# A third buffer for raw weight chunks and a shifted pace of decoding

## The chip, the core and the metric

The kernel runs on one core of a Trainium2 chip. The metric is the device time of one execution in microseconds; a kernel's time is the median over several executions. The engines are named as in the profile: PE is the matrix engine (PEld its weight loads), DVE the vector engine, ACT the scalar engine, POOL the GpSimd engine, SP the engine whose queue issues nearly all of this kernel's DMAs.

## The reference

Two blocks follow one another. Four batches of eight heads, 768 positions, 64 dimensions; a query sees the keys of its own cluster only; then a feed-forward layer with a hard-swish gate over 3072 tokens.

```python
def _attn_ref(q, k, v, centroids):
    q_n, k_n, c_n = ...                     # rows divided by their norms
    q_assign = np.argmax(np.einsum('bhsd,hcd->bhsc', q_n, c_n), axis=-1)
    k_assign = np.argmax(np.einsum('bhsd,hcd->bhsc', k_n, c_n), axis=-1)
    mask = q_assign[:, :, :, None] == k_assign[:, :, None, :]
    scores = scale * np.matmul(q, k.transpose(0, 1, 3, 2))
    scores = np.where(mask, scores, -1000000000.0)
    attn = np.exp(scores - np.max(scores, axis=-1, keepdims=True))
    attn = attn / (np.sum(attn, axis=-1, keepdims=True) + 1e-09)
    return np.matmul(attn, v)

def _moe_ref(x, w_in, w_out):               # (3072,512) (512,2048) (2048,512)
    h = x @ w_in
    g = h * np.clip(h + 3.0, 0.0, 6.0) / 6.0
    return g @ w_out
```

The weights `w_in` and `w_out` arrive as 64-bit floating-point numbers. The kernel reads them as pairs of 32-bit words and makes 32-bit floats of them: this is the decoding of which the change speaks.

## The kernel before

The heads are worked on in 16 pairs. A pair has 12 steps `n` (two halves of the queries, six chunks of keys in each), and the program's loop takes two steps at a time, so that `r = n % 12` is 0, 2, 4, 6, 8 or 10. The order of the instructions on each engine is the order in which this loop writes them out (`tc.manual_schedule`); semaphores between the engines are added to it. A batch is four pairs, 48 steps.

In each step PE forms the scores of 128 keys and 384 queries for two heads (`ps`, L418), ACT takes the exponentials (`ex`, L441), POOL sums them over the keys (`acc`, L461 and L464), and two steps later PE multiplies them with v (`pv`, L474). Once in six steps `divide` has PE add up the sums into one PSUM bank (`pd`, L495), DVE take the reciprocal (`rcp`, L499) and the product (`num`, L500). Then `keep` stores the result to DRAM (`xd`, L503) and lets ACT run the two activations of `in_range` over `rcp` (L512, L513); they come out one loop turn later. The preparation of the next pair lies between: transposes of q and k (`pqk`, copied to `xf`), scores against the centroids (`pcs`, copied to `cs`), their maximum and the one-hot rows on DVE (`mx` L337, `one_hot` L343), and the transposed one-hots (`po`, copied to `xm`). One PSUM pool, `psum_t`, has a single bank; from step 96 on `pd`, `pcs` and the other scratch tiles of the preparation share it.

The weights are 32 chunks of 128 x 512 numbers. `load_weights(i)` requests one chunk on SP's queue into a tile `raw` of pool `rawp` (L208). Five operations decode it: `split` (which also requests a further chunk, starts an activation on ACT that reads `raw`, L221, and a shift on DVE, L225), `join` (L231), `power` (a second activation, L237, and L241), `rest` (the last reader of `raw` on DVE, L247) and `total` (L252). After 160 of these come eight `weight_sums` (L547), which form sums of blocks of `w_out` for a fast matrix product after Strassen and Winograd. At the end of every turn of the loop, `share(n, r)` says how many of these 168 operations are written out:

```python
for step in decode[: share(n, r)]:
    step()
del decode[: share(n, r)]
```

`READY` is 56 and `DECODED` is 96. From step 60 to step 94 eight `up` items of the feed-forward layer are put in (`ph`, L613 on PE; ACT's `lift`, L523; DVE's `clip`, L526; four POOL sums of the results, L648). They read `xb`, a block that SP loads back from `xd` (L561). From step 96 on the decoding is over, four steps are written out together, and the first `down` items form the products `X` and `Y` (L693), along with which `make_first_sums` writes sums of `w_in` (`tx`, L580) on DVE.

All of this is the program's fast path. A general path for inputs outside its assumptions follows behind a branch; with these inputs it isn't run.

Of the kernel before, what the change touches and what calls it, by code (L numbers as in the profile page):

```python
# [116 lines left out]
def fast_path(ctx, tc, ok, q, k, v, centroids, moe_w_in, moe_w_out, out):  # L117
# [23 lines left out]
    dram = pool("dram", 1, space=bass.MemoryType.DRAM)  # L141
    yp = pool("yp", 1)
    decoding = ctx.enter_context(ExitStack())
    rawp = decoding.enter_context(tc.tile_pool(name="rawp", bufs=2))
    decp = decoding.enter_context(tc.tile_pool(name="decp", bufs=2))
    startp = decoding.enter_context(tc.tile_pool(name="startp", bufs=1))
    psum_s = pool("psum_s", 2, space=PSUM)
# [26 lines left out]
    def scratch(shape, name, dtype=F32):  # L174

        if st["early"]:
            return psum_m.tile(shape, dtype, name=name, tag="m")
        return psum_t.tile(shape, dtype, name=name, tag="t")
# [3 lines left out]
    def load(g, *names):  # L182
        if g >= NPAIR:
            return
        b, h = divmod(2 * g, H)
        for name in names:
            if name == "v":
                dst = st["v", g] = vp.tile([P, 2, NCH, D], F32, name="vt")
            elif name == "q":
                st["qk", g] = qkp.tile([P, 2, NCH, 2, D], F32, name="qk")  # L190
            if name != "v":
                dst = st["qk", g][:, "qk".index(name)]
            src = {"q": q, "k": k, "v": v}[name]
            for t in range(2):
                nc.sync.dma_start((dst[:, t] if name == "v" else dst[:, :, t]), src[b, h + t].rearrange("(p j) d -> p j d", p=P))
# [9 lines left out]
    def load_weights(i):  # L205
        if i < len(chunks):
            st["raw", i] = rawp.tile([P, WC, 2], U32, name="raw")
            nc.sync.dma_start(st["raw", i], chunks[i][1])  # L208

    def decoding_steps(i):  # L210

        got = {}

        def split():
            load_weights(i + 1)
            raw = st.pop(("raw", i))
            got.update(lo=raw[:, :, 0], hi=raw[:, :, 1])
            got["size"] = decp.tile([P, WC], BF16, name="wsize")
            got["top"] = psum_t.tile([P, WC], U32, name="wtop", tag="t")
            got["unit"] = decp.tile([P, WC], U32, name="wunit")  # L220
            nc.scalar.activation(  # L221
                out=got["size"], in_=got["hi"].bitcast(F32), func=ACT.Abs,
                accum_out=w_totals[:, 0, i : i + 1],
            )
            nc.vector.tensor_scalar(  # L225
                out=got["top"], in0=got["hi"], scalar1=3, scalar2=0x3FFFFFFF,
                op0=ALU.logical_shift_left, op1=ALU.bitwise_and,
            )

        def join():  # L230
            nc.vector.scalar_tensor_tensor(  # L231
                out=got["top"], in0=got["hi"], scalar=0xC0000000, in1=got["top"],
                op0=ALU.bitwise_and, op1=ALU.bitwise_or,
            )

        def power():
            nc.scalar.activation(  # L237
                out=got["size"], in_=got["size"], func=ACT.Relu, bias=w_low, scale=-1.0,
                accum_out=w_totals[:, 1, i : i + 1],
            )  # L240
            nc.vector.tensor_scalar(  # L241
                out=got["unit"], in0=got["top"], scalar1=0xFF800000, scalar2=None, op0=ALU.bitwise_and
            )

        def rest():
            unit = got["unit"].bitcast(F32)
            nc.vector.scalar_tensor_tensor(  # L247
                out=unit, in0=got["lo"], scalar=2.0**-52, in1=unit, op0=ALU.mult, op1=ALU.mult
            )

        def total():
            nc.vector.tensor_tensor(  # L252
                out=chunks[i][0], in0=got["top"].bitcast(F32), in1=got["unit"].bitcast(F32), op=ALU.add
            )

        return [split, join, power, rest, total]
# [8 lines left out]
    def constants():  # L265
        make_identity(nc, ident)
        for t in range(2):
            nc.vector.tensor_reduce(
                out=parity[:, t : t + 1],
                in_=ident.rearrange("p (h t c) -> p t h c", t=2, c=C)[:, t], axis=AX.XY, op=ALU.max,  # L270
            )
        nc.gpsimd.memset(half_c, 0.5)
        nc.gpsimd.memset(low_c, 1.0 / BOUND)
        nc.gpsimd.memset(ones, 1.0)
        nc.gpsimd.memset(w_low, W_LOW)
        nc.gpsimd.memset(one_hot, 0.0)
        for c in range(C):
            nc.gpsimd.memset(number[:, c : c + 1], float(c))

        warm = psum_t.tile([P, 4, P], F32, name="warm", tag="t")  # L280
        for i in range(14):
            nc.tensor.transpose(out=warm[:, i % 4], in_=ident, identity=ident)
# [36 lines left out]
    def cluster_scores(g):  # L319
        c0, xf = (2 * g) % H * C, st["xf", g]  # L320
        ps = scratch([P, 512], "pcs")[:, 0 : NC2 // 4 * P]
        for a in range(4):
            nc.tensor.matmul(  # L323
                ps[a * 2 * C : (a + 1) * 2 * C], lhsT=cnT[:, c0 : c0 + 2 * C], rhs=xf[:, a::4],
                start=True, stop=True,
            )
        cs = st["cs", g] = rtp.tile([P, NC2 // 4, P], F32, name="cs")
        nc.scalar.copy(out=cs, in_=ps)
# [81 lines left out]
    def scores_qk(n):  # L410
        st["ps", n] = psum_s.tile([P, 2, 512], F32, name="ps")
        scores_part(n, st["xf", where(n)[0]], True, by_vector(n))
# [402 lines left out]
    def share(n, r):  # L815

        if n < READY:
            return {0: 4, 2: 2, 4: 3, 6: 1, 8: 2, 10: 4}[r]
        return {0: 6, 2: 5, 4: 5, 6: 3, 8: 5, 10: 5}[r]

    def items_by(n):

# [56 lines left out]
    with tc.manual_schedule():  # L879
        nc.scalar.dma_start(cen, centroids.rearrange("h c d -> (h c) d"))  # L880
        load(0, "q", "k")
        constants()
        load(0, "v")
        load_weights(0)
        centroid_norm()
        for part in range(3):
            turn(0, part)
        centroid_turn()
        nc.vector.tensor_copy(out=ident_q, in_=ident)
        load(1, "q", "k")  # L890
        cluster_scores(0)
        scores_qk(0)
        route(0)
        scores_qk(1)
        for part in range(2):
            route_turn(0, part)

        for n in range(0, total + lag_d + 2, 2):
            g, r = divmod(n, per_pair)
            fours = n >= DECODED  # L900
            steps = [i for i in (n, n + 1) if i < total]
            prep = prep_items(g + 1, r, fours)
            if fours:
                four_by_four(n, r, steps)
            else:
                for i in steps:
                    scores(i)
                    exponentials(i)
                    key_sums(i)
                for i in (n - lag_v, n - lag_v + 1):  # L910
                    if i >= 0:
                        attn_v(i)
                m = n - lag_d + 1
                if m >= 0 and m % NCH == NCH - 1:
                    later.append(divide(m))
                    ready(m)
            if prep and r == (6 if fours else 4):
                prep.pop(0)()
            if n == DECODED:
                st["early"] = False  # L920
            if r == 6 and not fours:
                load(g + 2, "q", "k")
                load(g + 1, "v")
            if not fours or r % 4 == 2 or n >= total:
                want = min(items_by(n + 2) - st["done"], len(fill))
                st["done"] += want
                for i in range(max(len(prep), want)):
                    if i < want:
                        fill.pop(0)()
                    if i < len(prep):  # L930
                        prep[i]()
            if r == 6 and fours:
                load(g + 2, "q", "k")
                load(g + 1, "v")
# [3 lines that stand above are left out]
            if not fours:  # L938
                for op in numbers:
                    op()  # L940
                numbers.clear()
                check_all()
            checks.extend(later)
            later.clear()

        while checks:
            check_all()
            checks.extend(later)
            later.clear()
        st["last"] = True  # L950
        flag = whether_good()
        while fill:
            fill.pop(0)()
            if len(fill) == HOLD // 2:
                flag()
# [363 lines left out]
```

## Time and profile before

| | us |
|---|---|
| median of 8 runs | 1013.88 |
| lowest and highest | 1012.55, 1015.71 |
| the profiled execution | 1013.33 |
| its span, first to last instruction | 1011.5 |
| PE busy in the span | 987.9 |
| DVE, POOL, ACT busy | 564.3, 430.9, 390.2 |

Start and idle times in the text are microseconds from the start of the span. The profile comes from one execution. A wait is named after the instruction that waited and the one whose end released it. Busy times of PE include pipelining, so a PE that is busy throughout is not necessarily at its peak.

### The profile page before, as it was taken

How to read it: one execution, taken by the hardware profiler on the slowest of the kernel's cores; microseconds unless marked ns; L12 is line 12 of the kernel's file. 1: busy time of each engine (PE TensorE's matmuls, PEld its weight loads, DVE VectorE, ACT ScalarE, POOL GpSimd, SP SyncE). 2: the span in 40 equal slices, each digit the busy share in tenths (PEclk: the TensorE clock that was granted, in tenths of full speed). 3: DMA queues.
4: the chain of work that ended last, by engine and by line, in shares of the span. 5: the costliest groups of instructions: out<-in, count | busy, mean ns of one | idle time of the engine just before them, and what ended most of it. 6: DMA issues, size and time to landing. Idle time of an engine off the chain costs nothing.

```text
span 1011.5 us, 16735 instructions
## 1 busy us (share of the span) xinstructions
PE 987.9 (98%) x6560; PEld 734.6 (73%) x6560; DVE 564.3 (56%) x1085; ACT 390.2 (39%) x764; POOL 430.9 (43%) x363
## 2 busy tenths in 40 slices
PE   7999999999999999999999999999999999999997
PEld 4444445555688777788787777778777899999996
DVE  4888888988954255236236247147156372727270
ACT  6788877665233243233323333333223020201010
POOL 4877766665426326426415426515426130303030
PEclk9999999999999999999999999999999999999999
DMA  7334455432252052123223125023033041414120
GB/s 184 99 117 134 124 166 148 137 116 59 102 169 84 9 154 76 47 89 86 64 86 103 42 69 138 26 76 103 21 91 92 31 145 38 130 50 118 52 63 25
DMA packets 87560, 92.70 MB, mean 92 GB/s; under 512 B 53936, under 2 KB 68272, under 8 KB 87472
## 3 DMA queue, kind: packets, MB, share of 16 engines
q1 hardware_dynamic: 87328, 91.51, 31.4%
q8 instruction: 54, 0.88, 0.4%
q14 instruction: 34, 0.28, 0.1%
q10 hardware_dynamic: 144, 0.03, 0.0%
HBM read 75.79 MB, written 15.73 MB: 90 GB/s over the span
## 4 chain that ended last, share of the span: by engine, by line
PE 88%; DVE 6%; ACT 4%; issue 1%; DMA 1%; SPq 0%; ACTq 0%; DVEq 0%
PE Y L693 16%; PE uY L658 15%; PE ps L418 13%; PE X L693 12%; PE uX L658 12%; PE pv L474 11%; PE ph L613 2%; PE pd L495 2%; PE pqk L310 2%; DVE tx L580 1%; PE pcs L323 1%; ACT ex L441 1%; PE po L367 1%; DVE rcp L499 1%; ACT xm L369 1%
## 5 line engine op out<-in xcount | busy, mean ns | idle before, releaser
L464 POOL TENSOR_TENSOR acc<-acc,ex 128x768 f32<-128x768 f32 x128 | 241.6, 1887 | 130.9 <-ACT ex L441 124.2
L648 POOL TENSOR_TENSOR g_sb<-g_sb 128x256 f32<-128x256 f32 x176 | 127.9, 748 | 319.5 <-DVE g_sb L526 298.3
L441 ACT ACTIVATE ex<-ps 128x768 f32<-128x768 f32 x192 | 148.3, 804 | 85.1 <-PE ps L418 84.5
L523 ACT ACTIVATE sx<-g_sb,half_c 128x512 f32<-128x512 f32 x88 | 63.5, 722 | 268.3 <-DVE g_sb L669 268.3
L418 PE MATMUL ps<-xf 64*128 64x384 f32 x768 | 157.0, 487 | 0.8 <-ACT ex L441 0.8
L474 PE MATMUL pv<-ex,vt 128*64 128x384 f32 x768 | 141.1, 496 | 0.0
L700 DVE TENSOR_TENSOR y<-y,Y 128x256 f32<-128x256 f32 x48 | 20.2, 420 | 169.9 <-PE Y L693 169.1
L474 PEld LDWEIGHTS pv<-ex,vt 128*64 128x64 f32 x768 | 48.7, 136 | 82.4 <-issue 72.7
L499 DVE RECIPROCAL rcp<-pd 128x384 f32<-128x384 f32 x32 | 81.8, 2557 | 47.7 <-PE pd L495 46.8
L461 POOL TENSOR_TENSOR acc<-ex 128x768 f32<-128x768 f32 x32 | 59.6, 1861 | 99.6 <-ACT ex L441 99.6
L658 PE MATMUL uX<-xb,w_in_sb 128*128 128x128 f32 x704 | 93.0, 275 | 0.0
L693 PE MATMUL X<-w_out_sb,g_sb 128*128 128x256 f32 x384 | 89.7, 381 | 0.0
L693 PE MATMUL Y<-T,g_sb 128*128 128x256 f32 x384 | 87.3, 380 | 0.0
L693 PE MATMUL Y<-w_out_sb,g_sb 128*128 128x256 f32 x384 | 87.2, 380 | 0.0
L658 PEld LDWEIGHTS uX<-xb,w_in_sb 128*128 128x128 f32 x704 | 85.7, 192 | 0.0
L418 PEld LDWEIGHTS ps<-xf 64*128 64x128 f32 x768 | 67.7, 188 | 21.7 <-issue 18.0
L693 PEld LDWEIGHTS X<-w_out_sb,g_sb 128*128 128x128 f32 x384 | 71.2, 190 | 12.9 <-issue 3.5
L693 PEld LDWEIGHTS Y<-T,g_sb 128*128 128x128 f32 x384 | 72.3, 190 | 11.2 <-issue 1.7
L693 PEld LDWEIGHTS Y<-w_out_sb,g_sb 128*128 128x128 f32 x384 | 72.2, 190 | 11.1 <-issue 1.1
L526 DVE SCALAR_TENSOR_TENSOR g_sb<-sx,g_sb 128x512 f32<-128x512 f32 x88 | 67.3, 770 | 0.9 <-ACT sx L523 0.9
L418 PE MATMUL ps<-xm 64*128 64x384 bf16 x384 | 60.9, 327 | 6.5 <-ACT ex L441 3.4
L669 DVE TENSOR_TENSOR g_sb<-uY,sx 128x128 f32<-128x128 f32 (+1 forms) x176 | 65.6, 415 | 0.1
(110 smaller groups left out, 1379.5 us busy)
## 6 DMA issues: line engine op xcount, KB each, us to landing
tx<-td SPq DMA_DIRECT2D x86, 384.0 KB, 3.2
raw<-in_moe_w_in_dram SPq DMA_DIRECT2D x16, 512.0 KB, 4.0
raw<-in_moe_w_out_dram SPq DMA_DIRECT2D x16, 512.0 KB, 3.6
qk<-in_q_dram SPq DMA_DIRECT2D x32, 192.0 KB, 4.4
qk<-in_k_dram SPq DMA_DIRECT2D x32, 192.0 KB, 4.7
vt<-in_v_dram SPq DMA_DIRECT2D x32, 192.0 KB, 3.8
xd<-num SPq DMA_DIRECT2D x32, 192.0 KB, 2.9
xb<-xd SPq DMA_DIRECT2D x12, 512.0 KB, 4.2
```

The costliest lines, as they stand in the source:

```text
L418: nc.tensor.matmul(st["ps", n][:, t, 0:HALF], lhsT=x[r, NCH + j], rhs=x[r, hf * NHC : (hf + 1) * NHC], start=first, stop=last,)
L441: nc.scalar.activation(out=ex, in_=sc, func=ACT.Exp, scale=SM_SCALE)
L461: nc.gpsimd.tensor_tensor(out=acc, in0=st["ex", n - 1], in1=ex, op=ALU.add)
L464: nc.gpsimd.tensor_tensor(out=acc, in0=acc, in1=ex, op=ALU.add)
L474: nc.tensor.matmul(pv[t * D : (t + 1) * D], lhsT=vt[:, t, j], rhs=ex[:, t], start=(j == 0), stop=(j == NCH - 1),)
L499: nc.vector.reciprocal(out=rcp, in_=pd)
L523: nc.scalar.activation(out=r, in_=h, func=ACT.Relu, bias=half_c, scale=1.0 / 6.0)
L526: nc.vector.scalar_tensor_tensor(out=g, in0=r, scalar=1.0, in1=h, op0=ALU.min, op1=ALU.mult)
L648: eng.tensor_tensor(out=out_, in0=in0, in1=in1, op=op)
L658: nc.tensor.matmul(dst, lhsT=w[:, kt], rhs=x(kt), start=(kt == 0), stop=(kt == HK - 1))
L669: nc.vector.tensor_tensor(out=out_, in0=in0, in1=in1, op=ALU.add)
L693: nc.tensor.matmul(bank[:, half * HC : (half + 1) * HC], lhsT=g_sb[:, kind, i], rhs=w[:, i], start=(first and i == 0), stop=(last and i == ...
```

## The change

`rawp` gets a third buffer. `split` of chunk i requests chunk i + 2 instead of i + 1, and chunk 1 is requested before the loop, behind the q and k of pair 1. A request still waits until the chunk that last held its buffer has been read: that was chunk i - 1 before and it is chunk i - 1 now, but the chunk requested is needed five operations later than before. In the table of `share`, a pair has 17 operations instead of 16 before `READY` (one more at r = 2) and 28 instead of 29 from there on (one fewer at r = 4).

```diff
-    rawp = decoding.enter_context(tc.tile_pool(name="rawp", bufs=2))
+    rawp = decoding.enter_context(tc.tile_pool(name="rawp", bufs=3))
...
         def split():
-            load_weights(i + 1)
+            load_weights(i + 2)
             raw = st.pop(("raw", i))
...
         if n < READY:
-            return {0: 4, 2: 2, 4: 3, 6: 1, 8: 2, 10: 4}[r]
-        return {0: 6, 2: 5, 4: 5, 6: 3, 8: 5, 10: 5}[r]
+            return {0: 4, 2: 3, 4: 3, 6: 1, 8: 2, 10: 4}[r]
+        return {0: 6, 2: 5, 4: 4, 6: 3, 8: 5, 10: 5}[r]
...
         load(1, "q", "k")
+        load_weights(1)
         cluster_scores(0)
```

## The prediction

> **What bounds the kernel now.** I read the busy times first, then TensorE's own waits, then the chain of waits backwards from the two longest of them.
>
> ```profile
> PE 987.9 (98%) x6560; PEld 734.6 (73%) x6560; DVE 564.3 (56%) x1085; ACT 390.2 (39%) x764; POOL 430.9 (43%) x363
> ```
>
> PE is the bound, so a change outside PE pays only where PE stands idle. These are PE's waits between 10 and 290 us (total, times, longest):
>
> ```profile
> PE ps L418 <- ACT ex L441: 4.2, 6, 2.0
> PE ps L418 <- ACT xm L369: 2.8, 5, 1.3
> PE pcs L323 <- DVE rcp L499: 2.5, 1, 2.5
> PE pqk L310 <- ACT xf L312: 1.6, 2, 0.8
> ```
>
> The page's list for the whole span has the same totals, so after 290 us there is nothing of this kind. The decoding ends near 250 us. The timeline of PE places the waits (start, duration, and in brackets the idle time before):
>
> ```profile
> 191.03 0.34 PE L418 MATMUL ps<-xm 64*128 64x384 bf16 x2 [0.42 <-ACT ex L441]
> 229.96 0.34 PE L418 MATMUL ps<-xm 64*128 64x384 bf16 x2 [2.01 <-ACT ex L441]
> 271.54 0.85 PE L323 MATMUL pcs<-xf,cnT 128*32 128x384 f32 x8 [2.52 <-DVE rcp L499]
> ```
>
> The one at 229.96 is followed back in the chain of waits:
>
> ```profile
> 220.21 2.23 DVE wunit L247
> 222.50 3.83 DMA raw<-in_moe_w_out_dram
> 226.35 0.78 ACT wsize L221 x2
> ```
>
> The last raw chunk (31) could be requested only when `rest` of chunk 29 had freed its buffer at 222.45. It landed at 226.33, and ACT, which had reached this chunk's `split` at 221.35, stood still for 5.00 us, with the exponentials of step 90 queued behind it. From there DVE sets the pace:
>
> ```profile
> 231.60 0.69 DVE L526 SCALAR_TENSOR_TENSOR g_sb<-g_sb,ph 128x512 f32<-128x512 f32 x1 [2.61 <-ACT g_sb L523]
> 233.33 1.61 DVE L247 SCALAR_TENSOR_TENSOR wunit<-raw,wunit 128x512 f32<-128x512 uint32 x1
> 235.70 2.00 DVE L547 TENSOR_TENSOR T<-w_out_sb 128x1024 f32<-128x1024 f32 x1
> 242.72 4.62 DVE L547 TENSOR_TENSOR T<-w_out_sb,T 128x1024 f32<-128x1024 f32 x4
> 247.86 2.35 DVE L547 TENSOR_TENSOR w_out_sb<-w_out_sb 128x1024 f32<-128x1024 f32 x2
> 268.94 2.55 DVE L499 RECIPROCAL rcp<-pd 128x384 f32<-128x384 f32 x1
> ```
>
> Between 231.6 and 271.5 DVE has no idle time worth naming; PE was through with its work at 269.02 and waits for that reciprocal to give back its PSUM bank. So the reciprocal's end at 271.49 decides: time won upstream only lengthens this wait unless the DVE chain ends earlier too.
>
> **The change part by part.** The pace. Counting the tables, 145 decoding operations are out by step 82 (before: 142), 160 by step 88 (158), 163 by step 90 (161), and the last of the 168 at step 92 instead of 94. Nothing is added or removed; PE's order is the same.
>
> First five pairs (to 130 us): one operation more per pair, 0.73 us of DVE (starts of L225 to L231) and a fifth of ACT's 1.5 us per chunk. DVE idles about 2 us before the reciprocal of step 8 in each pair (waiting for `pd`), which covers it; uncovered it would cost 0.73 us a pair. I take 0.
>
> ACT, places where it holds PE. PE waits 0.42, 0.57 and 0.42 us (124.91, 158.91, 191.03) where step 4 of a pair issues both activations of a chunk, with the two of `in_range` behind them and then the exponentials. After the change step 52 and step 64 still have two; step 76 has one. One activation with its read is 0.7 to 0.8 us, more than 0.42: gain 0.42. Steps 22 (two for one, at r=10) and 72 (three for two, at r=0) get heavier, but before had two at steps 34 and 46 and three at step 84 without a PE wait of this kind: 0, at worst 0.57 each.
>
> The third buffer. Chunk 31 is now requested at step 84's `split` of chunk 29 and waits for `rest` of chunk 28, which in the new order stands before the clip at 211.3; it lands by about 215. ACT wants it near 219. The 5.00 us of ACT vanish; PE had been idle 2.01 of them: gain 2.01. The other DMA wait of ACT (1.07 us at 135.58) had no PE wait behind it: 0. On SP, each load still waits for the same kind of release as before, and behind it queue q, k, v loads, `xd` stores and the load of `xb` (issued 129.2). The release that counts there, at step 50, has one decoding operation more ahead of it: 0.7 us. `xb` takes 3.9 to 5.1 us and is wanted at 137.15, so some 3 us of slack cover it; beyond them every us is a us of PE. At the start, chunk 2 is requested at about 11 us instead of 17.7, just behind the k of pair 1. At the 289 GB/s seen there its 0.52 MB take 1.8 us; if all of it fell upon k, PE would lose up to 1.8 us near 15 us. As the k requests are in front, I take 0.
>
> The DVE chain, which decides. After the clip at 211.3 (now 210.9, PE being 0.42 ahead) come 6 decoding operations (4.4), reciprocal and product (2.57 + 1.30), 5 operations with one slow `rest` (5.1) and the last 4 (2.9 to 4.5): chunk 31 is finished at 227.8 to 229.4. `ph` is there at 227.15 and ACT, no longer held, lifts it by 227.8. Clip, maximum and one-hots take 1.7: the first weight sum starts at 229.6 to 231.2, against 235.70, 4.5 to 6.1 us earlier. Then three sums stand ahead of the reciprocal of step 92 instead of one: 2.00 + 2 x 1.155 (4.62/4) = 4.3; reciprocal and product 4.0; five sums 5.8; clip 0.6. That gives 244.3 to 245.9 for the first `tx` instruction, against 250.13.
>
> What may spoil it is POOL, with its sums of exponentials in the same stretch:
>
> ```profile
> 232.58 4.03 POOL L464 TENSOR_TENSOR acc<-acc,ex 128x768 f32<-128x768 f32 x2
> 236.79 4.46 POOL L464 TENSOR_TENSOR acc<-acc,ex 128x768 f32<-128x768 f32 x2 [0.18 <-ACT ex L441]
> 254.05 3.87 DVE L580 TENSOR_TENSOR tx<-w_in_sb,tx 128x256 f32<-128x256 f32 x2
> ```
>
> The first sum took 2.00 in there and 1.21 alone; the `tx` pair at 254.05 took 1.93 each where 0.43 is usual, one POOL sum apiece. But the two sums at 247.86 ran at full speed (2.35) while POOL's four L648 additions, started at 248.02, took 5.71 instead of 3.25: there POOL waited. Low end: only the first sum pays, as above. High end: all three pay a whole POOL sum, 3 x (1.89 + 1.21) = 9.3 instead of 4.3, and the 5.0 us eat the lead. I take the low end, because the neighbouring sums don't need each other's result, as those at 247.86, while each `tx` needs the one before.
>
> [...]
>
> From 244.3–245.9 the `tx` work runs on as before; POOL's pair that slowed it at 264 follows PE's exponentials and comes 2.4 earlier, when DVE is nearly through. So the reciprocal ends at 265.7 to 267.3 or sooner (its `pd` is ready at 262.3). PE arrives at 269.02 - 2.43 = 266.6. Of the 2.52 us, 0 to 0.7 remain; I take 0.2: gain 2.3. What is late next: in the new order the last clip stands behind all eight sums; PE wants its POOL products near 251.0 and they come by 247 to 249. After that PE is the bound as before.
>
> Sum: 0.42 + 2.01 + 2.3 = 4.7 us. The profiled execution took 1013.33 us (span 1011.5), so 1008.6; it lies 0.55 below the median of 1013.88, from which I forecast 1009.2.
>
> **The rivals.**
>
> A. Part is given back: the three sums delay reciprocal and product of step 92, whose `in_range` on ACT (242.40, with PE's lead 240.0) then waits, exponentials behind it; or pieces of the bounds above (k at the start, steps 22 and 72) come true. For it: the product ends at 237.9 to 239.5 in my sum, at up to 241.4 if one sum more pays. Cost 1.5 to 2.5, gain 2.2 to 3.2: about 1011.1.
>
> B. The DVE chain doesn't shift (high end of the POOL price): PE's 2.43 is lost at the reciprocal, whose wait grows from 2.52 to about 4.9. 1013.9. For it: the `tx` row at 254.05. Against: the row at 247.86, and 2.3 us of decoding that leave the chain.
>
> C. Slower. The mechanism: three sums ahead of step 92's reciprocal, each behind a POOL sum, without a lead of the decoding (if DVE's earlier waits, 3.76 us before 211.3 and 2.61 before 231.6, are not filled). The first sum then starts at 233.4, three take 9.3, the reciprocal ends at 245.3, product, five sums and clip at 253.1, 3.0 later than 250.13, and so is the reciprocal at 268.94. It decides once the first `tx` starts after 250.2. 1016.9. Against: DVE has operations ready for those waits.
>
> That the buffer does nothing is no rival of weight: the load of chunk 31 hangs on a release 11 us earlier.
>
> **How the numbers follow.** Forecast 0.65, A 0.16, B 0.11, C 0.08. Two microseconds are 0.2%, about what a measurement of this kernel can tell from no change. Faster: 0.65 and most of A, 0.78; same: B and a little of A, 0.14; slower: C, 0.08. The forecast's own range goes from 1007.8 (4.95 us gained, 0.4 for one of PE's waits for `xm` or `xf` closing too, 0.7 for the spread of a median) to 1010.2. A reaches to 1011.7; with half a microsecond of spread the whole range is 1007.8 to 1012.2, and B and C, 0.19, are left out.
>
> **What would show it.** Right: no wait of ACT for raw near 226; PE waits at 191 and 230 gone; first sum near 230; pcs L323 waiting under 0.7 us near 267. Wrong: the pcs wait at 2.5 us or more (B); sums at 2 to 3 us each with POOL between (A, B); a PE wait behind L512 near 240 (A); waits for q, k or `xb` near 15 or 137 us.

## The result, and the profile after

The changed kernel takes 1011.93 us (median of 12 runs, 1011.14 to 1013.14) beside 1014.62 us for the kernel before (32 runs, 1011.78 to 1016.72): ratio 0.9978, 95% interval 0.9968 to 0.9987. It is faster, by 2.2 to 2.7 us where 4.7 were forecast. The profiled execution took 1011.50 us, its span 1009.6 (before: 1013.33 and 1011.5). Executions of one kernel differ by some us, for two reasons given at the end, so traces are compared over one stretch: from the first `ps` of step 54, where PE waits 0.4 us in every kernel (124.91 before, 124.89 after), to the first `uX` (283.12 and 281.08). That stretch takes 158.21 us before and 156.19 after, 2.02 less; behind it PE's waits are the same in both.

The busy times after (engine, us, share of the span):

```profile
PE 988.4 (98%) x6560; PEld 734.1 (73%) x6560; DVE 568.9 (56%) x1085; ACT 390.1 (39%) x764; POOL 431.1 (43%) x363
```

PE is still the bound. DVE is 4.6 us busier with the same 1085 instructions: some of them ran slower. PE's waits between 10 and 290 us (total, times, longest):

```profile
PE ps L418 <- ACT xm L369: 2.5, 4, 1.3
PE po L367 <- DVE rcp L499: 2.2, 2, 1.8
PE ps L418 <- ACT ex L441: 1.7, 4, 0.6
PE pqk L310 <- ACT xf L312: 1.6, 2, 0.8
PE pqk L310 <- DVE rcp L499: 0.7, 1, 0.7
```

The wait for `ex` fell from 4.2 to 1.7 and the 2.5 of `pcs` are gone. New are three waits for a reciprocal, under `po` and `pqk`. PE's timeline places them:

```profile
183.30 0.66 PE L310 MATMUL pqk<-ident,qk 128*128 128x128 f32 x4 [0.73 <-DVE rcp L499]
...
199.39 0.49 PE L367 MATMUL po<-ident_q,one_hot 128*128 128x128 bf16 x6 [0.40 <-DVE rcp L499]
...
241.73 0.49 PE L367 MATMUL po<-ident_q,one_hot 128*128 128x128 bf16 x6 [1.83 <-DVE rcp L499]
```

Neither `po` nor `pqk` reads `rcp`. They want a PSUM bank: up to step 96 `scratch` takes its tiles from `psum_m`, which has two banks, and `pd` keeps one of them until the reciprocal has read it (e9 below puts this to the test for step 92). Compared point by point along PE, the trace gives this ledger (change of PE's lead in us, idle time and the restart behind it):

| place before / after | what happens | us |
|---|---|---|
| 191 / - | wait for `ex` behind step 76 gone | -0.49 |
| 230 / - | wait for `ex` behind ACT's wait for chunk 31 gone | -2.07 |
| 271 / - | wait of `pcs` for `rcp` of step 98 gone | -2.58 |
| 203 and 243 | two waits for `ex` and `xm` shorter or gone | -0.36 |
| - / 183 | `pqk` waits for `rcp` of step 74 | +0.93 |
| - / 199 | `po` waits for `rcp` of step 80 | +0.56 |
| - / 242 | `po` waits for `rcp` of step 92 | +1.99 |
| sum | | -2.02 |

So 5.5 us were gained and 3.5 given back. ACT's timeline shows the 5.00 us of waiting for chunk 31 gone (nothing in brackets):

```profile
218.99 0.66 ACT L221 ACTIVATE wsize<-raw 128x512 bf16<-128x512 f32 x1
```

DVE's timeline in the stretch that decided before:

```profile
229.26 0.69 DVE L526 SCALAR_TENSOR_TENSOR g_sb<-g_sb,ph 128x512 f32<-128x512 f32 x1 [0.51 <-ACT g_sb L523]
...
230.99 5.46 DVE L547 TENSOR_TENSOR T<-w_out_sb 128x1024 f32<-128x1024 f32 x2
236.38 2.83 DVE L547 TENSOR_TENSOR T<-w_out_sb,T 128x1024 f32<-128x1024 f32 x1
239.13 2.54 DVE L499 RECIPROCAL rcp<-pd 128x384 f32<-128x384 f32 x1
...
248.46 0.42 DVE L580 TENSOR_TENSOR tx<-w_in_sb 128x256 f32<-128x256 f32 x1
...
265.32 2.56 DVE L499 RECIPROCAL rcp<-pd 128x384 f32<-128x384 f32 x1 [1.24 <-PE pd L495]
```

The first weight sum starts at 230.99 instead of 235.70. But the three sums ahead of the reciprocal run to 239.13, 8.1 us, with POOL's sums of exponentials beside them all the time:

```profile
230.81 4.57 POOL L464 TENSOR_TENSOR acc<-acc,ex 128x768 f32<-128x768 f32 x2 [3.33 <-ACT ex L441]
235.59 5.28 POOL L464 TENSOR_TENSOR acc<-acc,ex 128x768 f32<-128x768 f32 x2 [0.22 <-ACT ex L441]
```

`pd` was ready at 232.6 and PE wanted its bank back at 239.9; the reciprocal began at 239.13 and gave it at 241.67. The last reciprocal, of step 98, is through at 267.9 and PE comes to `pcs` only at 269.51.

### The profile page after: what moved, and what is told of

Same layout as the page of the kernel before. It is cut to its first block, busy times and chain, and to the rows that moved or that the text cites. A ratio compares the mean times of both kernels' runs of the same rounds, so it can differ in the third digit from the quotient of the medians.

```text
span 1009.6 us, 16725 instructions
## 1 busy us (share of the span) xinstructions
PE 988.4 (98%) x6560; PEld 734.1 (73%) x6560; DVE 568.9 (56%) x1085; ACT 390.1 (39%) x764; POOL 431.1 (43%) x363
## 4 chain that ended last, share of the span: by engine, by line
PE 76%; DVE 2%; ACT 1%; issue 0%; ACTq 0%
PE Y L693 17%; PE uY L658 15%; PE X L693 12%; PE uX L658 12%; PE ps L418 9%; PE pv L474 7%; PE pd L495 1%; PE pqk L310 1%; PE ph L613 1%; PE pcs L323 1%; PE po L367 1%; DVE T L547 1%; DVE g_sb L526 0%; DVE sx L669 0%; DVE one_hot L343 0%
## 5 line engine op out<-in xcount | busy, mean ns | idle before, releaser
L648 POOL TENSOR_TENSOR g_sb<-g_sb 128x256 f32<-128x256 f32 x176 | 126.2, 738 | 320.3 <-DVE g_sb L526 299.0
```

What stands on the lines that cost most here:

```text
L648: eng.tensor_tensor(out=out_, in0=in0, in1=in1, op=op)
```

## The experiments

Theory: the forecast's gains are real, and the new tables give part back, as `rest` and weight sums that run beside POOL come ahead of three reciprocals, each of which holds one of two PSUM banks. Rivals: the late reciprocals hold PE up another way (`in_range` on ACT, rival A of the prediction); the sums are slow for another reason than POOL; one part of the change makes the other superfluous. Ratios below are to the kernel before in the same series, with 95% intervals; "stretch" is the time defined above.

| kernel | median us | ratio | stretch us |
|---|---|---|---|
| the change | 1011.93 | 0.9978 (0.9968 to 0.9987) | 156.19 |
| the change again (e8) | 1013.64 | 0.9987 (0.9975 to 1.0000) | 157.85, 1.65 of it slow clock |
| buffer alone (e1) | 1009.12 | 0.9943 (0.9927 to 0.9959) | 153.54 |
| buffer alone again (e11) | 1009.26 | 0.9943 (0.9928 to 0.9959) | 153.53 |
| tables alone (e2) | 1013.71 | 0.9993 (0.9983 to 1.0002) | 157.91, 1.41 of it slow clock |
| one sum ahead of step 92 (e3) | 1011.51 | 0.9961 (0.9946 to 0.9976) | 154.48 |
| steps 74 and 80 relieved (e4) | 1010.51 | 0.9960 (0.9945 to 0.9976) | 156.57, 1.61 of it slow clock |
| both (e5) | 1010.51 | 0.9949 (0.9933 to 0.9965) | 153.21 |
| without POOL's sums (e6) | 1011.99 | 0.9970 (0.9959 to 0.9981) | 154.49 |
| another bank for `pd` (e9) | 1012.32 | 0.9975 (0.9965 to 0.9986) | 155.00 |
| buffer, step 76, first try (e7) | 1009.21 | 0.9949 (0.9936 to 0.9962) | 153.56 |
| buffer, step 76 (e10) | 1008.71 | 0.9935 (0.9919 to 0.9951) | 153.10 |

"Slow clock" is what the way from PE's wait near 242 to `uX` takes over the 39.35 us of the first profile of the change. The intervals of the buffer alone, e5, e7 and e10 lie clear of that of the change; for the other kernels the times don't decide, and the readings below rest on one trace each.

**The buffer alone (e1, and again e11).** Against the changed kernel:

```diff
-            return {0: 4, 2: 3, 4: 3, 6: 1, 8: 2, 10: 4}[r]
-        return {0: 6, 2: 5, 4: 4, 6: 3, 8: 5, 10: 5}[r]
+            return {0: 4, 2: 2, 4: 3, 6: 1, 8: 2, 10: 4}[r]
+        return {0: 6, 2: 5, 4: 5, 6: 3, 8: 5, 10: 5}[r]
```

> The changed kernel with the old table of decoding operations (16 and 29 to a pair): the third buffer alone. My theory: the changed kernel wins 4.9 us at three waits of PE (191, 230, 271 us) and gives 3.0 back at three new waits for a late reciprocal, whose PSUM bank in psum_m PE wants (0.73 at 183, 0.40 at 199, 1.83 at 242 us). The first two come from where the new pace lays the slow rest operations, the third from three weight sums ahead of the reciprocal of step 92. With the old pace only one sum stands there, so none of the three new waits appears; the wait for raw (2.01 at 230) is gone, the 0.42 at 191 stays, and at 271 between 0.5 and 2.5 us are left, as two decoding operations stay in the DVE chain. Total 2 to 4 us faster than before, as fast as the changed kernel or up to 1.5 us faster. Rival (the pace does the work, the buffer is of no account): the wait at 230 stays near 2 us and the total is that of before. Rival (the buffer itself costs, by its early loads): a new wait of PE before 130 us.

> The third buffer with the old tables once more, on the same chip as the changed kernel. Theory 1 (the shifted pace gives back some 3 us): ratio 0.9935 to 0.9955, lower than that of the changed kernel by 0.002 to 0.003; 153.4 to 153.7 us from the first ps of step 54 to the first uX. Theory 2 (the first series differed by chip or by the pace of TensorE's start): a ratio within 0.001 of that of the changed kernel.

Measured: the old pace with the third buffer is the faster kernel, on two chips at the same ratio, with an interval that doesn't meet that of the change. Its stretch is 4.67 and 4.68 us shorter than before: 2.07 and 2.58 from the places at 230 and 271. PE's waits in the second of these profiles:

```profile
PE ps L418 <- ACT xm L369: 2.8, 5, 1.3
PE ps L418 <- ACT ex L441: 2.2, 5, 0.6
PE pqk L310 <- ACT xf L312: 1.6, 2, 0.8
PE po L367 <- DVE one_hot L343: 0.3, 1, 0.3
```

No reciprocal is among them. The gain is larger than expected for e1 (5.2 us against 2 to 4), as nothing of the wait at 271 is left, and the ratio lies 0.0044 below that of the changed kernel, more than the 0.002 to 0.003 expected for e11. What follows: nearly the whole gain is the buffer's, and the tables take some 2.6 us of it away.

**The tables alone (e2).** Against the changed kernel, two buffers and a request one chunk ahead:

```diff
-    rawp = decoding.enter_context(tc.tile_pool(name="rawp", bufs=3))
+    rawp = decoding.enter_context(tc.tile_pool(name="rawp", bufs=2))
...
-            load_weights(i + 2)
+            load_weights(i + 1)
...
-        load_weights(1)
```

> Two buffers and a request one chunk ahead as before, with the changed tables alone. Theory 1 (the tables alone already do away with ACT's wait for chunk 31, so that in the changed kernel the buffer no longer matters): chunk 31 is requested when `rest` of chunk 29 has ended, near 215.8 us instead of 222.45, lands by 219.6, ACT wants it at 219.0 and waits 0.6 us at most; the three PE waits for a late reciprocal (near 183, 199 and 242 us; 0.7, 0.4 and 1.8 us) stand as in the changed kernel; from the first ps of step 54 to the first uX 156.0 to 156.6 us (before 158.21, changed 156.19); ratio to the kernel before 0.997 to 0.999. Theory 2 (the buffer is what takes the wait away): ACT waits for raw by 3 us or more and PE by 1.5 us or more behind it, and with the three reciprocal waits the kernel is at 1.000 to 1.003.

Measured: ACT's activation of chunk 31 has no wait at all (its timeline), and PE's three waits for a reciprocal stand, the last of them as long as in the change:

```profile
222.18 0.68 ACT L221 ACTIVATE wsize<-raw 128x512 bf16<-128x512 f32 x1
```

```profile
244.73 0.49 PE L367 MATMUL po<-ident_q,one_hot 128*128 128x128 bf16 x6 [1.83 <-DVE rcp L499]
```

Theory 1 holds. Decoding two operations earlier brings the request of chunk 31 forward by itself, so each part of the change removes the same 5.00 us of ACT. Together they gain it once, and pay for the tables. Without the 1.41 us of slow clock the stretch would be 156.5 us, in theory 1's range; the ratio of the medians is just above it.

**Which operations hold the reciprocals (e3, e4, e5).** The changed kernel with single steps of the table set by hand: e3 has one operation instead of three at step 90, so one weight sum ahead of the reciprocal of step 92; e4 moves `join` and `power` of chunk 24 from step 72 to 74 and `rest` and `total` of chunk 26 from 78 to 80, behind the reciprocals there; e5 does both.

```diff
+        moved = {90: 1}                               # e3
+        moved = {72: 4, 74: 7, 78: 1, 80: 7}          # e4
+        moved = {72: 4, 74: 7, 78: 1, 80: 7, 90: 1}   # e5
+        if n in moved:
+            return moved[n]
```

> The changed kernel with one decoding operation instead of three at step 90, so that one weight sum stands ahead of the reciprocal of step 92 instead of three, and the two others behind it (two come out at step 94, behind the last clip, as before). My theory (bank held by a late reciprocal): the reciprocal starts near 233 instead of 239.1, PE's wait at 242 (1.83) is gone, those at 183 and 199 stay; the pcs wait near 270 stays under 0.6. 1.3 to 2.0 us faster than the changed kernel. Rival (the DVE chain decides as a whole): DVE has the same work up to 265, so the 1.8 us come back as the pcs wait near 268, and the total is that of the changed kernel within 0.5. Rival (ACT's in_range behind the product): same time gain, but then PE's wait would have been put down to ACT, and ACT shows no wait at L512 in the changed kernel.

> The changed kernel with two decoding operations moved from step 72 to step 74 and two from step 78 to step 80, that is from ahead of a reciprocal to behind it; the lead at all other steps is the same. My theory: the reciprocals of steps 74 and 80 start 1.4 to 3 us earlier (180.7 to about 179, 196.8 to about 195), PE's waits at 183 (0.73) and 199 (0.40) are gone, that at 242 stays. 0.9 to 1.2 us faster than the changed kernel, if no wait of ACT comes up by three activations at step 74. [...] Rival (the DVE chain decides as a whole): the lateness comes back at the clip of step 84 or at 242, no gain.

> Both edits in one: operations moved behind the reciprocals of steps 74, 80 and 92. My theory: the three new waits of PE are gone, the three gains stay; 2.4 to 3.2 us faster than the changed kernel, 4.5 to 5.5 faster than before. This is the 4.7 us of the prediction, got by another way. Rival (DVE chain as a whole): no more than e3 or e4 alone, the rest coming back as the pcs wait near 267.

Measured: in e3 the wait near 242 is gone and those of 0.76 and 0.39 us for steps 74 and 80 stay; in e4 these two are gone and 1.84 stays; in e5 all three are gone. The stretch is 154.48, 156.57 less 1.61, and 153.21 us. What follows: each wait hangs on the work that DVE has ahead of that reciprocal, and they add up. By the rows the reciprocals of steps 74 and 80 came late by `rest`: of the five between 170 and 197 us three take 2.13, 2.17 and 1.97 us in the change (175.74, 188.08, 194.18), each begun 0.2 to 0.4 us behind one of POOL's sums (175.51, 187.87, 193.78); before, none of the five takes over 1.17. That POOL made these slow is read from the rows and not shown by a run: e4 takes other work out of the way at step 74 and leaves the slow `rest` in its place (2.15 us in e5, which has the same operations there). The medians of e4 and e5 are equal, 1010.51; there the traces decide, not the times.

**POOL left out (e6).** Against the changed kernel:

```diff
-        elif j > 1:
+        elif j > 1 and not 92 <= n < 96:
```

> The changed kernel with POOL's four additions of exponentials (L464) of steps 92 to 95 left out; the sums of those keys are so left out of the result. Theory 1 (POOL's additions make the three weight sums slow, and these the reciprocal late): the three L547 sums ahead of the reciprocal of step 92 take 3.5 to 4.4 us together instead of 8.29, the reciprocal ends near 237.5 instead of 241.67, PE's wait of 1.83 us for it at 241.73 is gone, from the first ps of step 54 to the first uX 154.2 to 154.7 us instead of 156.19; ratio 0.995 to 0.9965. Theory 2 (the sums are slow for another reason, or the wait isn't theirs): sums at 7 us or more, the wait at 1.5 us or more, 156 us, ratio 0.997 to 0.9985.

Measured, on DVE's timeline:

```profile
233.54 2.35 DVE L547 TENSOR_TENSOR T<-w_out_sb 128x1024 f32<-128x1024 f32 x2
235.81 1.22 DVE L547 TENSOR_TENSOR T<-w_out_sb,T 128x1024 f32<-128x1024 f32 x1
236.95 2.55 DVE L499 RECIPROCAL rcp<-pd 128x384 f32<-128x384 f32 x1
```

The same three sums take 3.4 us instead of 8.1, PE's 1.83 us are gone and the stretch is 154.49 us, in theory 1's range. The ratio, 0.9970, is 0.0005 above its range, at the lower end of theory 2's, and doesn't decide. The 4.7 us are POOL's.

**Another bank (e9).** Against the changed kernel; no instruction moves:

```diff
-        pd = scratch([P, 512], "pd")
+        pd = psum_t.tile([P, 512], F32, name="pd", tag="t") if n == 89 else scratch([P, 512], "pd")
```

(`divide` counts by its last key step, 89, which is the call in step 92.)

> The changed kernel with `pd` of step 92 alone in the bank of psum_t, which is free by then, instead of one of the two banks of psum_m. No instruction is added, removed or moved. Theory 1 (PE waits at 241.73 only because `pd` holds one of the two banks that `po` needs): the three sums take 8 us and more as before, the reciprocal still ends at 241.5 to 241.8, but PE's 1.83 us are gone or under 0.2; PE then reaches pcs of step 98 near 267.7, as that reciprocal ends at 267.9, and waits 0.1 to 0.5 there; from the first ps of step 54 to the first uX 154.4 to 154.9 us instead of 156.19; ratio 0.995 to 0.997. Theory 2 (the late reciprocal holds something else up too, such as the activations of `in_range` and the exponentials behind them): a PE wait of 1 us or more stays near 242, named after another releaser; 155.7 us or more, ratio 0.997 to 0.9985.

Measured, on DVE's, ACT's and PE's timelines (all of this execution is 1.14 us later than in the change):

```profile
240.31 2.54 DVE L499 RECIPROCAL rcp<-pd 128x384 f32<-128x384 f32 x1
```

```profile
243.48 0.52 ACT L512 ACTIVATE rcp<-rcp 128x384 f32<-128x384 f32 x1 [0.98 <-DVE num L500]
```

```profile
240.91 0.50 PE L367 MATMUL po<-ident_q,one_hot 128*128 128x128 bf16 x6
...
245.58 0.34 PE L418 MATMUL ps<-xm 64*128 64x384 bf16 x2 [0.45 <-ACT ex L441]
```

The reciprocal is as late as ever (240.31 less 1.14 is 239.17), and `po` no longer waits: the bank was what held PE. Behind it a second, shorter way shows: `in_range` waits 0.98 us for the product, the exponentials stand behind it, and PE loses 0.45; a wait of 0.30 for `xm`, which the kernel before has there too, is back as well. So the stretch is 155.00, 0.1 above theory 1's range, and both theories have a part: the bank first, ACT's way of rival A next in line. The ratio, 0.9975, lies in theory 2's range and doesn't separate this kernel from the change.

**The wait behind step 76 (e7, e10).** With the buffer alone one wait of the forecast's sum remains, 0.42 us at 191. Against the buffer alone:

```diff
+        moved = {76: 4, 78: 4}   # e7
+        moved = {76: 3, 78: 5}   # e10
+        if n in moved:
+            return moved[n]
```

> The third buffer with the old tables, and one decoding operation moved from step 76 to step 78, so that step 76 issues one activation less. Theory 1 (the old tables with the buffer leave only PE's wait of 0.42 us behind step 76, and nothing takes its place): that wait under 0.1, no PE wait for a reciprocal, from the first ps of step 54 to the first uX 153.0 to 153.3 us (the buffer alone 153.54); ratio 0.9935 to 0.9950. Theory 2 (the operation moved delays the reciprocal behind it): a PE wait of 0.3 to 0.7 us for rcp near 185, 153.5 to 154.0 us, ratio 0.9945 to 0.9960.

> The third buffer with the old tables, and two decoding operations moved from step 76 to step 78, so that step 76 issues one activation instead of two (the single operation moved in the run before was `rest`, which has no activation). Theory 1 (the second activation is what PE waits for behind step 76): the wait of 0.41 us is gone, no PE wait for a reciprocal comes up, from the first ps of step 54 to the first uX 153.0 to 153.3 us (the buffer alone 153.54); ratio to the kernel before 0.993 to 0.995. Theory 2 (the wait there hangs on `in_range` and the exponentials alone, or the two operations come back as a wait behind step 78): a PE wait of 0.3 us or more between 189 and 201 us, 153.4 to 154.0 us, ratio 0.9940 to 0.9955.

Measured: e7 kept the wait (0.43 us), since the operation moved was `rest`, and the step still issued two activations: a miss of the experiment's edit. In e10, with one activation in step 76, the wait is gone, nothing takes its place, and the stretch is 153.10 us, 0.43 less than with the buffer alone. This is the fastest kernel of all, 0.9935; its time alone doesn't separate it from the buffer alone.

**The two kernels once more (e8, e12).**

> The changed kernel once more, on the same chip as the buffer alone. Theory 1: ratio 0.9965 to 0.9985, and 156.1 to 156.3 us from the first ps of step 54 to the first uX, or up to 1.6 us more where the granted clock falls behind PE's wait near 242. Theory 2: a ratio within 0.001 of the buffer alone.

> The kernel before once more, for a second profile. Three of the four profiles in which PE waits 1.83 us near 242 us show a granted clock of 0.58 to 0.66 over the four microseconds behind it, and some 1.5 us lost; none of the eight without that wait does. Theory 1 (any PE wait of about 2 us can bring this on): the waits of 2.01 near 230 and 2.52 near 271 of the kernel before do it too in some executions; if this profile is one, the window behind one of them has a clock under 0.8 and the profiled time is 1014.5 to 1017. Theory 2 (it belongs to the place near 242 alone, or to the tables): clock 1.00 in both windows, and the time is 1011.5 to 1014.5, set by the pace of the start.

The changed kernel came out at 0.9987, above the buffer alone by 0.0044 in one series and 0.0002 above theory 1's range. Its second profile has the same three waits, and behind the last of them PE's instructions between 245.66 and 249.82 take longer: `pv` 2.31 instead of 1.51 us. The table of windows (us of PE, PEld, DVE, ACT and POOL busy, the granted clock, DMA) has 0.60 there:

```profile
246.00:250.00 4.00, 4.00 (x20) 1.45 (x18) 4.00 (x4) 2.38 (x7) 0.00 (x0) 0.60 0.15 50
```

The kernel before, in its second profile, does the same behind its wait of 2.02 us at 230.07 (windows, clock 0.82 and 0.75) and loses 1.65 us by 235.5:

```profile
228.00:232.00 4.00, 1.98 (x11) 1.33 (x12) 1.32 (x3) 3.97 (x10) 1.20 (x1) 0.82 0.70 175
232.00:236.00 4.00, 4.00 (x24) 1.33 (x22) 3.90 (x7) 1.20 (x2) 3.84 (x3) 0.75 0.00 0
```

So theory 1 holds as to the mechanism, and its time (1014.5 to 1017) doesn't: this execution took 1012.86, in theory 2's range. The reason is on DVE's timeline. In the first profile of before, POOL's pair at 264.18 met the `tx` sums:

```profile
263.75 2.54 DVE L580 TENSOR_TENSOR tx<-w_in_sb,tx 128x256 f32<-128x256 f32 x2
266.21 2.02 DVE L580 TENSOR_TENSOR w_in_sb<-w_in_sb 128x256 f32<-128x256 f32 x1
```

In the second one PE, and so POOL, came 1.8 us later, and missed them:

```profile
264.69 0.89 DVE L580 TENSOR_TENSOR tx<-w_in_sb,tx 128x256 f32<-128x256 f32 x2
265.49 0.42 DVE L580 TENSOR_TENSOR w_in_sb<-w_in_sb 128x256 f32<-128x256 f32 x1
...
266.61 2.55 DVE L499 RECIPROCAL rcp<-pd 128x384 f32<-128x384 f32 x1
```

The reciprocal ended at 269.2, before PE came to `pcs` at 270.71: the wait of 2.52 us didn't exist in this execution. It was the price of one meeting, 3.3 us long: without it the reciprocal of the first profile would have ended at 268.2, before PE came at 269.02.

## Why the prediction was half right

**ACT behind step 76**: forecast 0.42, found 0.49 in the change and 0.43 by itself in e10. Right.

**ACT's wait for chunk 31**: forecast 2.01, found 2.07, and 2.07 with the buffer alone. Right. What the text missed is that the tables alone remove it as well (e2).

**The reciprocal of step 98**: forecast 2.3 of 2.52, found 2.58, by another way than the one worked out. The first `tx` was to start by 245.9 and started at 248.46; that was enough, as POOL's pair no longer met the `tx` sums. The buffer alone does it too (e11), with the reciprocal through at 265.60 and PE at `pcs` at 266.89, with the old tables: as ACT is no longer held, DVE's clip comes at 228.93 instead of 231.60 and the first `tx` at 247.50 instead of 250.13. The sum "that decides" was not needed for its result.

**The step that failed** is the price of the three weight sums: "Low end: only the first sum pays ... I take the low end". It gave 4.3 us; the sums took 8.1, near the high end of 9.3, and 3.4 when POOL was silent (e6). The first sum began in the forecast's range (230.99 in 229.6 to 231.2), so this term alone made the reciprocal of step 92 late: with 4.3 us it would have ended at 237.8, before PE wanted the bank at 239.9. It was argued from two sums that had run undisturbed at 247.86, beside another POOL instruction. The nearer row was the first sum, beside the very POOL sums that the next two would meet: 2.00 against 1.21. The row at 247.86 doesn't even hold for its own place. In the second profile of before, on DVE's and POOL's timelines, the same two sums took 2.88 us instead of 2.35, and POOL's four additions 5.04 instead of 5.71:

```profile
248.68 2.88 DVE L547 TENSOR_TENSOR w_out_sb<-w_out_sb 128x1024 f32<-128x1024 f32 x2
```

```profile
248.84 5.04 POOL L648 TENSOR_TENSOR g_sb<-g_sb 128x256 f32<-128x256 f32 x4 [6.30 <-DVE g_sb L526]
```

**The step that was missing** is what a late reciprocal holds. The text followed DVE's delay to `tx`, to `pcs` and, in rival A, to `in_range`; it knew the bank of `psum_t` behind step 98, and didn't ask which bank `pd` holds before step 96. By the bank the delay at step 92 costs PE 1.83 us; by `in_range` alone 0.45 (e9). For the same reason the tables were costed at ACT only, beyond the first five pairs, and the reciprocals of steps 74 and 80, with 1.5 us, are in no term.

**The rivals.** A has the right delay (three sums ahead of step 92's reciprocal), the nearest time (1011.1) and the wrong victim. In B the `tx` chain was not to move; it came 1.7 us earlier. C needed the decoding to bring no lead, and the first sum came 4.7 us earlier.

The forecast of 1009.2 us is what the buffer alone takes (1009.12 and 1009.26). Its three terms, 4.7 us, are met by e10, 5.11 us in the trace: they belonged to a change that leaves the reciprocals where they are.

## What to carry to other kernels

Before DVE work is moved ahead of an instruction that frees a PSUM bank, ask who allocates from that pool next, and follow the bank as well as the value. Where two engines' tensor operations have once slowed one another in a row of the trace, let every instruction that will lie in the same stretch pay that price (here the first sum took 2.00 us against 1.21, and the three took 8.1 against 3.4), and take a row from elsewhere only with a reason why it is the same case. A row of one execution may fall otherwise in the next, so look at a second profile before a sum rests on it. If two parts of a change remove the same wait, build each alone: here the buffer brings nearly the whole gain, and the tables beside it mostly cost.

## What the runs showed of the hardware

**PE's clock fell behind waits of about 2 us in four of six profiles.** Of the six profiles with a PE wait of 1.8 us or more between 180 and 280 us, four have a granted clock below 1.00 in windows of four microseconds behind it and lose 1.41 to 1.65 us: the second profile of the change (0.60 from 246 to 250), the second of before (0.82 and 0.75 from 228 to 236), e2 (0.66 from 246 to 250) and e4 (0.58 from 242 to 246). The first profiles of the change and of before have the wait and not the loss: their clock is 1.00 from 180 to 280 us. None of the eight profiles without such a wait has a clock under 1.00 in the windows read between 180 and 280 us. So in these four executions a wait of 1.83 to 2.02 us cost 3.2 to 3.7 us with the loss behind it, which may be why the buffer alone gains 5.2 and 5.9 us in the medians and 4.7 in the trace; that was not tested by itself. What decides which executions pay is not shown by any run.

**PE's start has two paces.** Step 54's first `ps` comes at 124.8 to 125.0 us in six profiles and at 126.0 to 127.6 in eight; the change and the buffer alone each have one of both kinds. The difference arises before 16 us, in the same matmuls. In the first profile of the change:

```profile
5.14 0.85 PE L310 MATMUL pqk<-ident,qk 128*128 128x128 f32 x6 [0.54 <-DMA qk<-in_q_dram]
...
8.64 0.85 PE L323 MATMUL pcs<-xf,cnT 128*32 128x384 f32 x8 [0.48 <-DVE ident_q L889]
```

and in its second profile:

```profile
5.01 1.51 PE L310 MATMUL pqk<-ident,qk 128*128 128x128 f32 x6 [0.40 <-DMA qk<-in_q_dram]
...
9.42 1.50 PE L323 MATMUL pcs<-xf,cnT 128*32 128x384 f32 x8 [0.48 <-DVE ident_q L889]
```

This `pcs` takes 0.85 us in the five early profiles whose start was read and 1.50 or 1.51 in the four late ones. The granted clock reads 1.00 in both profiles of the change from 0 to 15 us; the clock record in the trace of the first begins only at 5.1 us, so that ahead of it the 1.00 is no measurement. What sets the pace is not shown by any run. Profiles of a kernel this close to another are to be compared from an instruction behind the start.

**POOL and DVE took turns in the rows read here.** In the change each of the three sums lasts 2.7 to 2.8 us beside POOL's, 1.2 without (e6), and POOL's own sums, taken in pairs, last 2.3 to 2.6 us each instead of the 1.9 usual. By the single ends in the trace each of the three DVE sums is through 1.08 us after the POOL sum before it, and the POOL sum that follows 1.7 us after that. Where POOL's four L648 additions begin 0.16 us behind the first of the last two weight sums, the two sums take 2.35 us and the additions 5.71 in two profiles (before, e1); in before the first addition alone lasts 3.12 us, past the end of both sums. In three others (before again, e3, e5) the sums take 2.88 and the additions 5.04 or 5.05. What decides between the two stays open.
